# Softmax rows scaled at the evacuation of x instead of at P, by way of DRAM

## The chip, the cores and the metric

The kernel runs on one core of a Trainium2 chip. The metric is the device time of one execution in microseconds (us). The core has TensorE (PE, with its weight loads PEld), VectorE (DVE), ScalarE (ACT), GpSimd (POOL), and SyncE (SP), which in this kernel issues nearly all DMA transfers.

## The reference

Attention with a threshold for 8 batches of 8 heads (576 rows, head size 64), whose output x (4608 x 512) goes through a feed-forward layer that takes the maximum of three products.

```python
scores = scale * np.matmul(q, k.transpose(0, 1, 3, 2))
thresh = np.max(scores, axis=-1, keepdims=True) - tau          # tau = 0.02
scores = np.where(scores >= thresh, scores, -1000000000.0)
attn = np.exp(scores - np.max(scores, axis=-1, keepdims=True))
attn = attn / (np.sum(attn, axis=-1, keepdims=True) + 1e-09)
x = np.matmul(attn, v)                                          # (B, H, S, D) -> (B*S, H*D)
h = np.maximum(np.maximum(x @ w1, x @ w2), x @ w3)              # w: 512 x 768
out = h @ w_out                                                 # 768 x 512
```

## The kernel before

The work is cut into **quads**: 16 of them, two to a batch, each of four heads (two couples r = 0, 1). A quad's rows come as nine chunks (idx 0 to 8) of 128 rows; a chunk has two halves of 576 columns, one for each r. So there are 288 halves and 144 chunks. In the last batch (SPLIT) the rows are worked off in two parts.

A half goes through these steps. `scores` multiplies q and k on PE into a PSUM bank (sc). `maximum` on DVE copies it to a tile z and takes the row's minimum of the negated scores (nm). From there the table MASKED decides, one digit for each half:
- 0 and 2: `threshold` (only for 0, a small DVE instruction), then `exponents` on ACT flattens what lies under the threshold, then `numerators` on ACT takes the exponential and its row sum (letter n).
- 1 and 3: `exponents` on ACT takes the exponential, then `numerators` on DVE (SCALAR_TENSOR_TENSOR) masks it and sums the row (letter k).

2 and 3 read the scores from PSUM, 0 and 1 from z. Then `reciprocals` (DVE, one instruction for a chunk) and `normalized` (POOL, one instruction for each half) write P = z times the reciprocal sum in bf16, and `turned` transposes P by DMA into the tile ptq. When all chunks of a quad are there, `product` multiplies v with ptq on PE, once for each r, and x's quarter is copied from PSUM to the tile xt: on DVE for r = 0, on ACT for r = 1. `ffn` makes the hidden pieces of a batch (`hid`: bank ph, 6 x 3 of them; each has two halves on PE, letters F and B; ACT copies the first of three, DVE takes the two maxima) and then the output pieces (`outp`: bank po).

There are four PSUM banks for all of this. z has 9 buffers (ZBUFS) and, from the 73rd half on, also the two buffers of the weight stage (MORE_Z, `half_of_z`); P has 6.

The order on every engine is written out by hand in the string ORDER. A letter issues the next step of its kind, and each engine executes its own instructions in the order in which they appear: S, T, O, F, N (with the number of a bank) are PE's scores, transposes, products, feed-forward pieces and ninth rows; B is the second half of a piece; m maximum, s threshold, e exponents, n and k numerators, r reciprocals, p normalized, t the DMA transpose, a and c the evacuations of q and k, q their swapped copies, w and x the evacuations of x (DVE, ACT), h and v those of the hidden pieces (ACT, DVE), u, j and f those of the output, l, g, o, i, d the loads and stores, y and z POOL's casts. The class `_Ordered` (line 93, the line of nearly all rows of the profile) ties each instruction to the one before it on its engine.

Of the kernel before, what the change touches and what calls it, by code (L numbers as in the profile page):

```python
# [15 lines left out]
OP = AluOpType  # L16
# [5 lines left out]
FLAT = 2.0 ** -100  # L22

MASKED = """
232222322322222222021032222202332122123122200200111000000000100000000011
000010111020011000101000000001100001001000010011111100000000100100000000
110010030111000100010000000001010100001110001011010100110000000000000000
100101101011000000120000001010000000110011100000001110001000010011111021
# [6 lines left out]
MORE_Z = 72  # L35
# [5 lines left out]
llllllglllT0laclT1laclzllqqS0qqS1meS2mS3lmlT0enlkS1ylmlT2eamelrnpS3leqlmnyS1qcapS0emtnrcS3pmnT2qmepgrelS1qya  # L41
gS0pmelT2mqnS3tcpemqS2nlkT1eytaS0rmnT1kpermS3yS2enczrmS1qT0enmepnqtS3nprmaymgpeS0lptS2mppT0mtpS1enencnqsS3re
rmtpS0mS1penmS3lqnsS2mtperpekzllmT0tmpenkT1pgS3eearnS0petmnqrS2meqlnpS3lmnplsS2cetpremS1pS0nmplermtzeS3mnS2p
mtnpmS3rkpS1leektS0emnrpmemptS1eekS2pO3mktS0rennmpermT2pnS1wptemS3prkyO0tmeakS2pgS1enxlnrmS0lpesS2mezT3mS1np
mgntspcS2eqrseT3mtpeS0srmapS1mnT2ptS3mnqO0ceqmeO1prswnptnkS3pxS0meF1meS2zBresmT0qghF3klpF2nkBtaS1sveS0pemF3B
nyrrsmyBepT1svS0hpcT2nS3zmaS1erpgsF2mntpsBmnS3yvF1etssT0myeBprS2cnpS3mnS0ympelF2epF3lmBnzslssvS0htBrqmeS2vpn
S1gF0sepmF3teqBmF2erssvpBtnBkphF0eS1vtS3znmF2nrBmqteS1rpvBnS3pmlnF0pmgeS1qsBsrhmS3pevS2npS1mF0npsO3ermpesmO2
zewepgsskBxtT3nF1vS2nklBarS0mlphS3mtepF2sS1rmnyBmetF3pvT0eBpcnS2tzT1nvS0asmzS3temS2qeS1meF0trkpmS3lenpBmnlys
reklpF1umerpskS3upBeoketmS0uS2umpS3tesmS1qeT0myO2nqlrsnlprcO3etqsmepwS0xptS1mnF3psnmS2BlerskpS1thF0meF3pmeBF
2ktnBveBsrS1nvpS0hmyF3emF2npBrssT0eprtvBaF1kS3nqvBeF0myhyS2kyleF3mBelBvnpS2snsS0vptemS1pnF3rmpT2tnBmpeF0scS1  # L50
htBrnmpF3erT2rpvlBasS1pstvnS2pmeF0pS3emtBqnmT2S1hcqS3empF2eS0rsqmtS1epsmBeF3pmnF0stsvBeBknF2klhF1BvelS0nrvpB
emT3pS2arvS0ptnS3mpnO1smtesrkpeF2swnlrpmeT0S1qtescS3epBmnpmnT0trskS3paS1umS0ulqmeS3lmyS1nopS2smelS0rmeS3psmn
O1ypersmqO2etkpemO0lewqxlknpS3tS1keF2momS3lexF0ktT1enkBercpnsBpumN1ertkphkF3jS0rursS1empBnmF2ptS0vpS1smeF3yt
BsnsmBpnvS0pT1hmF2atT3srepS0cF1eprBsmeqF3vnByBynvplS2nsS0plmhS1mteS2mF0nF3mteS1rrspBnmS2pelvBlepF1smT0leqBvl
aS2rkhF3oqnsS0mtS1epmBeqsF2ssmtS0epvBeyF1mnF3vpBesrS0ktphBermS1npT2svO0nytmpncT3eS1wF2nrmS0aBrsmnqF3vnT1pS0c
eBptsF2mhpS1eS3pmteS0qmBeO1spmnkteF3rvnpT0BsskapS2xvS0erS1qmtnS3pmnF2mqlespmeS1rtkBepresmT3puS1cuS0ptmnS3pS2
meyS1lrekpF0tnsmempO3lekteskO2nrsmpeBkpxrnwS1uptS3muS2pnmF0yoeS1mF3lesymBtnS2srkpS1hmBeF0spveF2ertBmpT3nrsvS
1paBlmpnS0tS3qhmF1epsmS2leBymF3tevF0nBknlS1rsvpS2esmqnBF3srmhpS1epS0tmeF2pssBrempBtesvS0ynF1mT3lnpBvF0lhsrcS
2tnT1mBnF3valS2nrBsqmeF0pvS1epS2meBptsmS3eqF1hmT2peBcS3tnskT2O0arkplnmO2lerpvewptS3xkpS1nF2meF0sstreBsmpS3nv
pBnmS1tS2hmT3eF0rmpnF1cBpnBrevptT3S2apvS0qmtS3S1enmqF2esrsqmiepmleS0soykeS1plBnmemtS3ukS0uT1snrlO2cpekynO1me  # L60
ymeF3pwxskteS0keS1BrrnkopmF2pmS0BqeuurtsmF1phS3srnpS2meT0ptBmeS3ykpaN2esvempF0tS1jkpF3ermBeS2ptvnS1pmBnS0rls
hsmpS2elF3mqntS1mpF0nsrBskpeF2lsmBetBpveF1yhvS3lnkS2lesF0mytnBmBerqsS3veF2lpvnF1pBsmT0htBceF3rT2vnpBsaS0pvnF
1qmtS2nBsrnmT0pS3hrcpF2esS1mpteS0rmpS3emBpntF1svqnS0ssBmpeoT2vO3lamtneF1wS0nrlBpmeS3qsrS2hsmS0pnmF1eptS3smeB
pmF2ntS0veS3rsmnpS1BnpO0veytrempS2empS3xsmS1tekF0nsknlT2rmpBelmlpnscS3quS1umyS2eorT0kpeO3tmeyO1ewlepsmF3etka
rknS2qklT0nBmxespcS2eryF0mpF1uskpuBtnS2BhmqF3nsvS0peS2srmtpF1eBmpeF0srvnBptS2hyS3pmeF1lmeBlBevtF3nkT2S0arrvp
BnS2mphS1smpF0ntS3smnpBmeF1lsT2esvlF3nrBrcptBnvpS2eS0qmlhS1tsnprsmT3F2epmS0aptBemF3yevS1oS0nqmBnpsrS2mnF1ptv
S0epmBeS3mthS2skeF0F1snmlBeklO3ersvpnrmByepF0swT2eqtBvnqF3ssrcS1hpiBmpT0S2vaptS1snmS0pnT3mqF2tecT1BarmS3pnS1
vqeS0mF2pesrmnptmS3npT1seS0qctBeymqermpS1eS3mpuF0nmtuskS1eS2klnS3smBesrsepO1upmemO2txrkpukeO3wnkpS0xS2emF3et
rmS1pnBssspmF2hS0rtepS3mnBpmF1etS0veF3mnN2rnpBpjF0evtF2esBkBkhF1nsvS3eBmBevO3hrkS2pwnS1mnF3prmS2eptsF0mnBpsS
1sevyS2terBmpeF3svS1iyepBmoS0yhmtF2ekF3nBsmS1ersBvpnF0pmeF2BvteS1hBmF3rsS0vpeF1rknpBBmnO2vhptO0xrpnS3pwS2trm  # L70
npS0mnF3pmteF1pBeBvtS0rS2vpS3empF1ktkF0kBereskpemBkperumO2uptO3xpN1wtenkO2jrF3pxF1hpF2nvF3tvF1rhF2pvF3pvF1hF
2tvF3vF1hF2voF3vF1ohF2vF3vF1hF2vO3vO1wF2xuuF1oF0hiF3vF1vF0hF3vF1vF0hF3vF1vF0hF3vF1vF0hF3vF1vF0huF3vF1ovF3uoF
0uoN1fjdi
# [31 lines left out]
def kernel(  # L105
# [44 lines left out]
    def weight_loads():  # L150


        def piece(dst, src):
            my = {}

            def load():
                my["t"] = stage.tile([128, 4 * 256], F32, name="stage")
# [19 lines left out]
    small = ctx.enter_context(tc.tile_pool(name="small", bufs=6))  # L177
# [177 lines left out]
    halves_of_z = iter(range(1 << 20))  # L355

    def half_of_z():

        n = next(halves_of_z)
        if n >= MORE_Z and (n - MORE_Z) % (ZBUFS + 2) >= ZBUFS:  # L360
            return stage.tile([128, 4 * 256], F32, name="stage")[:, :S]
        return zz.tile([128, S], F32, name="z")

    def maximum(c, r):

        z = c["z", r] = half_of_z()
# [8 lines left out]
    def threshold(c, r):  # L375
        th = c["th", r] = small.tile([128, 1], F32, name="th", bufs=5)
        vector.tensor_scalar(out=th, in0=c["nm", r], scalar1=-1.0, scalar2=tau, op0=OP.mult, op1=OP.subtract)
# [22 lines left out]
    def normalized(c):  # L400
        c["P"] = P = pp.tile([128, W], BF16, name="P")
        for n in range(2):
            pool.tensor_scalar(out=P[:, n * S:(n + 1) * S], in0=c["z", n],
                                    scalar1=c["rs"][:, n:n + 1], scalar2=1.0, op0=OP.mult, op1=OP.mult)
            if n:
                line["t"].append(c)
            yield
# [7 lines left out]
    def product(L, r, target, part=None):  # L415
# [26 lines left out]
        def on_vector():  # L442
            ps = st["ps"]
            dst = target(L["b"])[:, 2 * L["qd"] + r, :]
            vector.tensor_copy(out=dst[:, lo:hi], in_=ps[:, base:base + hi - lo])

        def on_scalar():
            ps = st["ps"]
            dst = target(L["b"])[:, 2 * L["qd"] + r, :]
            scalar.activation(out=dst[:, lo:hi], in_=ps[:, base:base + hi - lo], func=AF.Copy)  # L450
        p = _Piece((L["b"], L["qd"], r, part), first)
        p.vector = on_vector if r == 0 else None
        p.scalar = on_scalar if r == 1 else None
# [25 lines left out]
    def ffn(b, part):  # L479
# [87 lines left out]
        def ninths_of_two():  # L567
# [11 lines left out]
            def done():  # L579
                ob = hp_.tile([128, DM], F32, name="ob9", bufs=1)  # L580
# [12 lines left out]
        def ninth():  # L593
# [10 lines left out]
            def done():  # L604
                ob = hp_.tile([128, DM], F32, name="ob9", bufs=1)[:, 0:DM // 2]
# [36 lines left out]
    Ls, xts, stores, stores9, ends, ninths = {}, {}, [], [], [], []  # L642
# [20 lines left out]
    vector.memset(vrs[2], 0.0)  # L663
    for t in vrs[0:2]:
# [33 lines left out]

    def flow(what, fn):
        while True:  # L700
            yield from fn(line[what].pop(0))
# [5 lines left out]
                O=products(), F=pieces(), N=iter(lambda: ninths.pop(0), None))  # L707
    line = {k: [] for k in "menkrptahvuxwcqsjf"}
    casts = iter([w[1] for w in wl])
    loads = iter([w[0] for w in wl])  # L710
    flows = dict(p=flow("p", normalized), q=flow("q", lambda x: swapped(*x)),
# [7 lines left out]
    def issue(what, where):  # L719
# [10 lines left out]
        elif what == "O":  # L730
            p = next(todo["O"])
            p.first(where)
            for k, fn in (("x", p.scalar), ("w", p.vector)):
                if fn:
                    line[k].append(fn)
# [11 lines left out]
        elif what == "m":  # L747
            c, r = line["m"].pop(0)
            maximum(c, r)
            line["e"].append((c, r))  # L750
            if not masked(c["g"], c["idx"], r) and not direct(c, r):
                line["s"].append((c, r))
        elif what == "s":
            threshold(*line["s"].pop(0))
# [4 lines left out]
        elif what in "nk":  # L759
            c, r = line[what].pop(0)  # L760
# [69 lines left out]
```

## Time and profile before

| | |
|---|---|
| time, median of three runs | 447.64 us (447.23, 447.64, 447.99) |
| profiled execution: span from first to last instruction | 444.8 us (a time of its own is not listed for it) |
| PE busy | 422.4 us (95%) |
| DVE / ACT / POOL busy | 392.8 / 403.0 / 311.9 us |
| DMA | 88.5 MB, mean 199 GB/s |

How to read the rows: a group row has line, engine, operation, the tiles written and read, shapes and count; then the time in which the group was busy, the mean of one instruction in ns, and the idle time in front of them with what ended it. A timeline row has start, duration and instruction. A row of busy time by stretch has its length and, for each engine, busy time and count, then the granted clock of TensorE, the DMA engines' busy share (over 1 when transfers overlap) and GB/s. A DMA row has tiles, issuing engine, count, size and the median time from issue to landing. SPq is SP's queue: an instruction that issues a DMA.

### The profile page before, as it was taken

The page shows a single profiled execution, that of the slowest core. Times are in us where ns is not written, and L with a number is a line of the kernel's source. Part 1 is how long each engine was busy: PE and PEld are TensorE (multiplying, and loading weights), DVE is VectorE, ACT ScalarE, POOL GpSimd, SP SyncE. Part 2 cuts the span into 40 slices and gives each one's busy share as a digit, 9 for nine tenths or more (in the row PEclk, how much of TensorE's full clock was granted, in tenths as well). Part 3 has the DMA queues.
Part 4 walks back from the last instruction along what each step waited for, and adds up shares of the span by engine and source line. Part 5 has one row for each costly group of instructions (what it writes and reads, how often), then busy time and mean ns, then how long its engine had stood idle before and what let it go on. Part 6 is the DMA issues. An engine that isn't in the chain of part 4 may idle for free.

```text
span 444.8 us, 14254 instructions
## 1 busy us (share of the span) xinstructions
PE 422.4 (95%) x5188; PEld 320.2 (72%) x5190; DVE 392.8 (88%) x1228; ACT 403.0 (91%) x836; POOL 311.9 (70%) x420
## 2 busy tenths in 40 slices
PE   7767789999999999999999999999999999999996
PEld 6334347787788767787788777788688886787873
DVE  3887999999999999999999999998999998899642
ACT  3999999999999999999999999899999999987632
POOL 2799989997878687696785877676676685457400
PEclk8998999999999999999999999999999999999999
DMA  7999999999999999699899999989999977487633
GB/s 188 275 293 199 291 169 269 235 243 262 229 180 194 212 222 292 125 256 167 143 234 189 230 198 203 209 168 210 208 206 194 244 151 105 83 179 136 145 116 108
DMA packets 213959, 88.50 MB, mean 199 GB/s; under 512 B 189184, under 2 KB 202240, under 8 KB 213888
## 3 DMA queue, kind: packets, MB, share of 16 engines
q1 hardware_dynamic: 213360, 86.96, 95.9%
q8 instruction: 41, 0.67, 0.6%
q10 hardware_dynamic: 528, 0.62, 0.5%
q14 instruction: 30, 0.25, 0.2%
HBM read 35.65 MB, written 9.44 MB: 101 GB/s over the span
## 4 chain that ended last, share of the span: by engine, by line
PE 86%; ACT 5%; DVE 4%; issue 2%; DMA 1%; SPq 0%; DVEq 0%; ACTq 0%
PE ph L93 32%; PE sc L93 32%; PE po L93 10%; PE o L93 9%; ACT z L93 5%; PE tp L93 3%; DVE z L93 3%; DMA qm<-in_q_dram 1%; ACT qt L93 1%; SPq L93 0%; DVE xt L93 0%; DVE hm L93 0%; DVE stage L93 0%; DVE rs L93 0%; ACT ob L93 0%
## 5 line engine op out<-in xcount | busy, mean ns | idle before, releaser
L93 POOL TENSOR_SCALAR P<-z,rs 128x576 bf16<-128x576 f32 x250 | 200.6, 814 | 63.3 <-DVE rs L93 28.1
L93 DVE TENSOR_SCALAR_CACHE_REDUCE z<-sc 128x576 f32<-128x576 f32 x250 | 183.7, 750 | 14.8 <-PE sc L93 10.1
L93 PE MATMUL sc<-kt,qs 64*128 64x256 f32 (+2 forms) x640 | 182.6, 423 | 5.7 <-DVE z L93 2.3
L93 PE MATMUL sc<-kt,qt 64*128 64x320 f32 (+2 forms) x640 | 182.4, 433 | 5.2 <-ACT z L93 3.3
L93 PE MATMUL ph<-xt,w 64*128 64x288 bf16 (+2 forms) x2160 | 170.8, 283 | 0.1
L93 PEld LDWEIGHTS <-w 64*128 64x128 bf16 (+1 forms) x2160 | 130.1, 94 | 28.6 <-issue 4.3
L93 ACT ACTIVATE z<-z 128x576 f32<-128x576 f32 x174 | 117.6, 679 | 0.1
L93 PEld LDWEIGHTS sc<-kt,qs 64*128 64x128 f32 (+1 forms) x640 | 92.4, 180 | 25.7 <-DVE z L93 5.7
L93 ACT ACTIVATE z<-z,th 128x576 f32<-128x576 f32 x143 | 106.2, 769 | 5.0 <-DVE th L93 4.2
L93 PEld LDWEIGHTS sc<-kt,qt 64*128 64x128 f32 (+1 forms) x640 | 91.9, 179 | 19.7 <-ACT z L93 5.9
L93 DVE SCALAR_TENSOR_TENSOR z<-z 128x576 f32<-128x576 f32 x76 | 62.2, 830 | 0.5 <-ACT z L93 0.5
L93 PE MATMUL po<-wo,hT 64*128 64x512 bf16 (+3 forms) x454 | 53.5, 354 | 0.3
L93 POOL COPY qs<-qt 64x640 f32<-64x640 f32 (+3 forms) x66 | 43.0, 652 | 10.8 <-ACT qt L93 7.2
L93 ACT ACTIVATE z<-z,nm 128x576 f32<-128x576 f32 x68 | 50.6, 767 | 0.0
L93 DVE TENSOR_TENSOR hm<-ph,hm 128x576 bf16<-128x576 f32 (+2 forms) x54 | 37.0, 686 | 9.2 <-PE ph L93 8.9
L93 ACT ACTIVATE hm<-ph 128x576 bf16<-128x576 f32 (+2 forms) x54 | 31.8, 589 | 13.4 <-PE ph L93 12.8
L93 POOL TENSOR_SCALAR P<-stage,rs 128x576 bf16<-128x576 f32 x38 | 30.4, 804 | 19.3 <-ACT z L93 5.4
L93 PEld LDWEIGHTS <-hT 64*128 64x128 bf16 (+2 forms) x456 | 30.0, 95 | 16.5 <-issue 2.3
L93 DVE TENSOR_TENSOR hT<-ph,hm 128x576 bf16<-128x576 f32 (+2 forms) x54 | 37.0, 686 | 4.0 <-PE ph L93 2.3
L93 PE MATMUL o<-ptq,vb 128*64 128x64 bf16 (+2 forms) x544 | 39.0, 281 | 0.0
L93 ACT ACTIVATION_READ_ACCUMULATOR z<-z 128x1 f32 x174 | 34.3, 197 | 0.0
L93 PEld LDWEIGHTS <-vb 128*64 128x64 bf16 x544 | 23.3, 111 | 12.8 <-issue 4.9
(45 smaller groups left out, 431.6 us busy)
## 6 DMA issues: line engine op xcount, KB each, us to landing
vm<-in_v_dram SPq DMA_DIRECT2D x32, 256.0 KB, 4.8
qm<-in_q_dram SPq DMA_DIRECT2D x15, 512.0 KB, 5.0
km<-in_k_dram SPq DMA_DIRECT2D x15, 512.0 KB, 5.3
out_dram<-ob SPq DMA_DIRECT2D x14, 512.0 KB, 4.0
stage<-in_moe_w_dram SPq DMA_DIRECT2D x9, 512.0 KB, 5.2
ptq<-P SPq DMA_TRANSPOSE x144, 4.0
vr<-in_v_dram SPq DMA_DIRECT2D x16, 128.0 KB, 3.4
stage<-in_moe_w_out_dram SPq DMA_DIRECT2D x3, 512.0 KB, 4.9
```

The source lines that it names most:

```text
L93: ins = fn(*a, **kw)
```

## The change

P stays unscaled. `numerators` write their result straight into P in bf16 (on ACT or DVE), `reciprocals` are taken once for a quad (once for each part in the last batch), in a DVE tile `turn` that DVE turns in blocks of 32 x 32. The result is stored to DRAM (`scale_rows`, letter D), read back by two transfers so that 64 partitions each hold the same row of factors (`scale_tile`, letter R, into a buffer of the weight stage), and multiplied in when x is copied from PSUM, on DVE for both r (letter w). `normalized` on POOL (p), the copy on ACT (x) and the further z buffers of the stage are gone; the small output tile ob9 now uses a z buffer. A mode 4 (`by_pool`) is added to the code, but the new MASKED has no 4: its digits are 164, 87, 28 and 9 of 0, 1, 2, 3 (169, 78, 33 and 8 before). MASKED and ORDER are new throughout.

```diff
     def numerators(c, r):
-        z, acc = c["z", r], c["sm"][:, r:r + 1]
-        if masked(c["g"], c["idx"], r):
-            vector.scalar_tensor_tensor(out=z, in0=z, scalar=thr, in1=z,
+        z, p, acc = c["z", r], half_of_p(c, r), sum_of(c, r)
+        if by_pool(c, r):
+            scalar.activation(out=p, in_=z, func=AF.Exp, bias=c["nm", r], scale=-1.0, accum_out=acc)
+        elif masked(c["g"], c["idx"], r):
+            vector.scalar_tensor_tensor(out=p, in0=z, scalar=thr, in1=z,
                                         op0=OP.is_ge, op1=OP.mult, accum_out=acc)
         else:
-            scalar.activation(out=z, in_=z, func=AF.Exp, scale=-1.0 / FLAT, accum_out=acc)
-    def reciprocals(c):
-        c["rs"] = small.tile([128, 2], F32, name="rs")
-        vector.reciprocal(c["rs"], c["sm"])
-    def normalized(c):
-        c["P"] = P = pp.tile([128, W], BF16, name="P")
-        for n in range(2):
-            pool.tensor_scalar(out=P[:, n * S:(n + 1) * S], in0=c["z", n],
-                                    scalar1=c["rs"][:, n:n + 1], scalar2=1.0, op0=OP.mult, op1=OP.mult)
...
+            scalar.activation(out=p, in_=z, func=AF.Exp, scale=-1.0 / FLAT, accum_out=acc)
...
+    turns = [one.tile([128, 2, 32], F32, name=f"turn{x}") for x in range(2)]
+    def reciprocals(g, part, n):
+        L, t = Ls[g], turns[n % 2]
...
+        if part is None:
+            vector.reciprocal(new[:, :, f:f + 9], sums[:, :, f:f + 9])
...
+            vector.reciprocal(new[to, :, at:at + 1], sums[of, :, was:was + 1])
+        vector.transpose(t[:, 1, :], t[:, 0, :])
+        scales[g, part] = dict(t=t)
+    def scale_rows(g, part):
+        s = scales[g, part]
+        s["rows"] = rows.tile([32, 128], F32, name="rows")
+        sync.dma_start(out=s["rows"].rearrange("j (b t) -> b j t", b=4), in_=s["t"][:, 1, :])
+    def scale_tile(g, part):
+        s, (lo, hi) = scales[g, part], span(part)
+        n = hi - lo
+        s["R"] = stage.tile([128, W], F32, name="stage").rearrange("p (r n) -> p r n", r=2)[:, :, 0:n]
+        src = s["rows"].rearrange("j t -> (j t)")[0:2560].rearrange("(r i y) -> i r y", i=2, y=640)
+        o = 64 * ninth_first(Ls[g]["b"]) + lo
+        for i in range(2):
+            sync.dma_start(out=s["R"][64 * i:64 * i + 64],
+                           in_=src[i, :, o:o + n].unsqueeze(0).to_broadcast([64, 2, n]))
...
-        def on_vector():
-            vector.tensor_copy(out=dst[:, lo:hi], in_=ps[:, base:base + hi - lo])
-        def on_scalar():
-            scalar.activation(out=dst[:, lo:hi], in_=ps[:, base:base + hi - lo], func=AF.Copy)
+        def done():
+            vector.tensor_tensor(out=dst[:, lo:hi], in0=ps[:, base:base + hi - lo],
+                                 in1=scales[2 * L["b"] + L["qd"], part]["R"][:, r, :], op=OP.mult)
```

In the new ORDER a unit (a quad, or a quad's part in the last batch; 18 of them) has the letters r, D and R in this order, then O and w. Two passages of it, the 15th unit from its D on and the last one:

```
DsRnesevS0S3mtO1eemF2tBw
rvtF3tF1F0hvF3vF1F2vhF3F0DRvhvF1F3O0vovO3wwF1F0F2
```

More of the change, by code (lines that the diff above doesn't have):

```diff
@@ L353, in direct, with by_pool @@
         return by_mask[2 * number[c["g"], c["idx"]] + r] in "23"
[L355 to L362, printed above, removed]
+    def by_pool(c, r):
+        return by_mask[2 * number[c["g"], c["idx"]] + r] == "4"
     def maximum(c, r):
-        z = c["z", r] = half_of_z()
+        z = c["z", r] = zz.tile([128, S], F32, name="z")
         nm = c["nm", r] = small.tile([128, 1], F32, name="nm")
@@ L663 @@
     vector.memset(vrs[2], 0.0)
+    for t in turns:
+        vector.memset(t[:, 0], 1.0)
     for t in vrs[0:2]:
@@ L697, in products, with units @@
                         yield product(Ls[g], r, x_of, part)
+    def units():
+        n = 0
+        for b in range(B):
+            for part in parts_of(b):
+                for g in (2 * b, 2 * b + 1):
+                    yield g, part, n
+                    n += 1
     def flow(what, fn):
@@ L753, in issue @@
         elif what == "s":
[L754 removed]
+            c, r = line["s"].pop(0)
+            threshold(c, r)
+            if by_pool(c, r):
+                line["b"].append((c, r))
+        elif what == "b":
+            c, r = line["b"].pop(0)
+            set_apart(c, r)
+            line["X"].append((c, r))
         elif what == "e":
@@ L758, in issue @@
             line["k" if masked(c["g"], c["idx"], r) else "n"].append((c, r))
-        elif what in "nk":
-            c, r = line[what].pop(0)
-            if "sm" not in c:
-                c["sm"] = small.tile([128, 2], F32, name="sm")
-            else:
-                c["summed"] = True
-            numerators(c, r)
-        elif what == "r":
-            c = made[line["r"].append(0) or len(line["r"]) - 1]
-            assert c["summed"]
-            reciprocals(c)
-            line["p"].append(c)
+        elif what in "nkX":
+            numerators(*line[what].pop(0))
+        elif what == "r":
+            g, part, n = next(todo["r"])
+            reciprocals(g, part, n)
+            line["D"].append((g, part))
+        elif what == "D":
+            g, part = line["D"].pop(0)
+            scale_rows(g, part)
+            line["R"].append((g, part))
+        elif what == "R":
+            scale_tile(*line["R"].pop(0))
         elif what == "t":
```

144 lines of the change are left out of this document (84 added, 60 removed).

## The prediction

> **What bounds the kernel now.** I read the page first: the busy shares, the 40 slices, the chain that ended last.
>
> ```profile
> span 444.8 us, 14254 instructions
> PE 422.4 (95%) x5188; PEld 320.2 (72%) x5190; DVE 392.8 (88%) x1228; ACT 403.0 (91%) x836; POOL 311.9 (70%) x420
> PE   7767789999999999999999999999999999999996
> ...
> PE ph L93 32%; PE sc L93 32%; PE po L93 10%; PE o L93 9%; ACT z L93 5%; PE tp L93 3%; DVE z L93 3%; DMA qm<-in_q_dram 1%; ACT qt L93 1%; SPq L93 0%; DVE xt L93 0%; DVE hm L93 0%; DVE stage L93 0%; DVE rs L93 0%; ACT ob L93 0%
> ```
>
> The slices say where PE is not busy: the first seven and the last. Then the busy time by stretch, which puts microseconds on that.
>
> ```profile
> core 0: us, PE busy (x) PEld busy (x) DVE busy (x) ACT busy (x) POOL busy (x), PEclk, DMA share, GB/s
> 9.00:75.00 66.00, 52.07 (x475) 30.41 (x475) 58.34 (x176) 63.59 (x137) 58.23 (x77) 0.93 1.12 249
> 0.00:89.00 89.00, 72.23 (x723) 46.57 (x725) 73.79 (x229) 79.96 (x171) 72.36 (x102) 0.94 1.08 240
> ...
> 89.00:433.00 344.00, 342.74 (x4420) 269.48 (x4418) 316.18 (x995) 320.10 (x661) 239.51 (x319) 1.00 0.97 192
> ...
> 200.00:300.00 100.00, 99.00 (x1295) 77.63 (x1292) 95.44 (x302) 96.46 (x199) 73.11 (x98) 1.00 1.02 193
> ...
> 433.00:445.00 12.00, 7.44 (x50) 4.15 (x49) 2.88 (x6) 2.94 (x6) 0.00 (x0) 0.98 0.29 100
> ```
>
> PE idles 89.0 - 72.23 = 16.8 us before 89 us, 1.3 us in the 344 us after it, and 4.6 us at the end. The change adds no matmul and removes none, so PE's 422.4 us stay. Only those 22 us can shrink, and any new hold shows as new PE idle time. In the front (9 to 75 us) ACT is busy 63.6 of 66 us (96%), DVE 88%: ACT feeds PE there. The order of PE's pieces is nearly the old one: the first hidden piece comes after score 54 in both, hidden piece 18 after score 79 in both.
>
> **What the change takes away and adds, engine by engine.** The groups give the counts, the timeline the time from one start to the next, which is what an operation costs on a full engine (its record overlaps the next one's).
>
> ```profile
> L93 POOL TENSOR_SCALAR P<-z,rs 128x576 bf16<-128x576 f32 x250 | 200.6, 814 | 63.3 <-DVE rs L93 28.1 <-ACT z L93 11.6 <-DVE th L93 7.4
> L93 DVE SCALAR_TENSOR_TENSOR z<-z 128x576 f32<-128x576 f32 x76 | 62.2, 830 | 0.5 <-ACT z L93 0.5
> L93 DVE TENSOR_TENSOR hm<-ph,hm 128x576 bf16<-128x576 f32 x42 | 31.5, 751 | 0.8 <-PE ph L93 0.6
> L93 DVE RECIPROCAL rs<-sm 128x2 f32<-128x2 f32 x144 | 22.0, 157 | 2.0 <-ACT z L93 1.4 <-ACT stage L93 0.2
> L93 DVE CAST xt<-o 128x576 bf16<-128x576 f32 x14 | 10.5, 749 | 0.5 <-PE o L93 0.5
> L93 ACT ACTIVATE xt<-o 128x576 bf16<-128x576 f32 x14 | 9.0, 640 | 0.2
> ```
>
> ```profile
> 11.57 0.76 DVE L93 SCALAR_TENSOR_TENSOR z<-z 128x576 f32<-128x576 f32 x1
> ...
> 12.26 0.75 DVE L93 TENSOR_SCALAR_CACHE_REDUCE z<-sc 128x576 f32<-128x576 f32 x1
> ...
> 64.33 0.75 DVE L93 TENSOR_SCALAR_CACHE_REDUCE z<-sc 128x576 f32<-128x576 f32 x1
> ...
> 64.47 0.67 ACT L93 ACTIVATE z<-z 128x576 f32<-128x576 f32 x1
> ...
> 65.01 0.75 DVE L93 TENSOR_SCALAR_CACHE_REDUCE z<-sc 128x576 f32<-128x576 f32 x1
> ...
> 65.14 0.67 ACT L93 ACTIVATE z<-z 128x576 f32<-128x576 f32 x1
> ...
> 66.48 0.15 DVE L93 RECIPROCAL rs<-sm 128x2 f32<-128x2 f32 x1
> 66.56 0.13 DVE L93 TENSOR_SCALAR th<-nm 128x1 f32<-128x1 f32 x1
> ...
> 72.37 0.64 ACT L93 ACTIVATE xt<-o 128x576 bf16<-128x576 f32 x1
> ...
> 72.90 1.44 ACT L93 ACTIVATE z<-z,nm 128x576 f32<-128x576 f32 x2
> ...
> 73.06 0.67 PE L93 MATMUL ph<-xt,w 64*128 64x288 bf16 x8
> ```
>
> So an unmasked numerator (its sum included) costs ACT 65.14 - 64.47 = 0.67 us; a maximum costs DVE 65.01 - 64.33 = 0.68, a masked numerator 12.26 - 11.57 = 0.69, a reciprocal 0.08; an evacuation of x costs ACT 72.90 - 72.37 = 0.53.
> - POOL loses all 288 scalings (250 at 814 ns and 38 on the stage tile). It is on no chain, so this alone is worth nothing.
> - ACT loses 18 evacuations (16 of full width, 9 us) and 10 unmasked numerators (n: 202 to 192; 6.7 us).
> - DVE loses 144 reciprocals (11.5 us), gains 18 groups of two or three reciprocals and a turn (not in the trace; between 0.16 and 0.48 us each by the reciprocal's row, taken as 0.25: 4.5 us), 18 evacuations with a multiplication (like hm<-ph,hm, 0.751 us beside the cast's 0.749, so no dearer than a cast; 0.68 each: 11 us) and 10 masked numerators (7 us). The masked numerator's mean of 830 ns against 760 for an undisturbed one should fall when POOL is quiet (-6 us). In sum +5 us for DVE, -16 for ACT. Neither bounds after 89 us, so there it only adds slack.
>
> In the front it counts. Up to the 72nd score the old order has 51 unmasked numerators, 2 evacuations of x and 4 of hm on ACT; the new one has 43, none and 5: 8 x 0.67 + 2 x 0.53 - 0.53 = **5.9 us less ACT work**. DVE there: masked numerators 15 to 21 (+4.1), evacuations 2 to 4 (+1.4), reciprocals 32 to three groups (-1.8), one maximum fewer (-0.7), quieter POOL (-1): +2 us. ACT had about 89 us of work to that point (67 exponents and 51 numerators at 0.67, 18 evacuations at 0.53) and DVE about 78 (71 maxima and 36 further passes at some 0.68, 54 small ones at 0.08); now it is 83 and 80, so DVE is next, 3 us behind. Bounds of the gain: 5.9 us if both run without gaps, about 2 if two equally full engines lose 5% to waiting for each other. I take **-4.5 us**.
>
> **The new chain.** For each of 18 units (a quad, or its part in the last batch): reciprocals, a store of 16 KB (D), two reads of 295 KB (R), then the evacuation (w) on DVE, which is executed in order: everything queued behind w (maxima, masked numerators, the maxima of the hidden pieces) stands still until both reads have landed, and PE's four banks are not freed. D and R go through SP, also in order: R, 36 issues, sits there until D has landed, and the transposes and loads behind it wait too.
>
> ```profile
> vm<-in_v_dram SPq DMA_DIRECT2D x32, 256.0 KB, 4.8
> ...
> km<-in_k_dram SPq DMA_DIRECT2D x15, 512.0 KB, 5.3
> ...
> out_dram<-ob SPq DMA_DIRECT2D x6, 128.0 KB, 3.4
> out_dram<-ob SPq DMA_DIRECT2D x3, 256.0 KB, 2.4
> ...
> out_dram<-ob SPq DMA_DIRECT2D x3, 64.0 KB, 2.6
> ```
>
> ```profile
> 66.99 0.66 SPq L93 DMA_DIRECT2D stage<-in_moe_w_dram  x1
> ```
>
> ```profile
> L93 SPq DMA_TRANSPOSE ptq<-P x144: 1241/1432/4678, 17.6 to 418.9; - x144
> ...
> DMA to landing us min/median/max: 3.2/4.0/8.1
> ```
>
> ```profile
> SPq L93 <- POOL P L93: 130.9, 83, 6.0
> ```
>
> Neither transfer is in the trace. D: nearest is the 64 KB store, 2.6 us (2.4 to 3.4 by the stores). R: nearest is vm's 256 KB load, 4.8 us; a transpose of the same 295 KB has median 4.0, at least 3.2; the upper bound is km's 5.3. The second read is issued 0.66 us after the first. From D's start to usable factors: 2.6 + 0.66 + 4.4 = **7.7 us**, bounds 2.4 + 0.66 + 3.2 = 6.3 and 3.4 + 0.66 + 5.3 = 9.4. The issues' SP time (54 x 0.66 = 36 us) and the waits for D (18 x 2.6 = 47 us) fit into what SP no longer waits for POOL (130.9 us).
>
> What covers the 7.7 us is PE's work between D and w in the new order. By the chain's shares a score is 32% of 444.8 / 288 = 0.49 us, a half of a hidden piece as much (288 of them), a product 9% / 36 = 1.1 us, a half of an output piece about 1.3 us (10% over 28 such halves and nine single pieces). Counting letters, twelve units have 7 us or more (the first four among them, as PE idles there), and POOL's absence hurts nowhere. Short ones:
> - unit 15, "DsRnesevS0S3mtO1eemF2tBw": two scores, a product, two halves: 3.1 us. D can run at most 0.5 us ahead of its place, since a store stands before it. DVE is held 7.7 - 3.6 = 4.1 us.
> - unit 12: three scores, an output half, a product, 4 us; only the reciprocals stand before D, so it can go 2.4 us early: held 1.2. Unit 5: 6.3 us by DVE's own work: held 1.4. Units 9 and 14: covered within 0.4 us.
>
> What a hold costs PE is in the trace: one masked numerator took 2.60 us, and the only hole in PE's middle lies right there.
>
> ```profile
> 277.13 2.60 DVE L93 SCALAR_TENSOR_TENSOR z<-z 128x576 f32<-128x576 f32 x1
> ```
>
> 1.9 us more than 0.69 on DVE went with the 1.0 us that PE misses between 200 and 300 us, so about 0.9 us of a hold is absorbed. Unit 15 then costs 3.2 us, units 5 and 12 together 0.8: **+4.0 us**.
>
> - The tail (unit 18, "DRvhvF1F3O0vovO3ww"). Nothing but the last part's hidden pieces follows, and they need x.
>
> ```profile
> 423.77 0.61 PE L93 MATMUL o<-ptq,vb 128*64 128x256 bf16 x8
> ...
> 424.58 1.47 PE L93 MATMUL po<-wo,hT 128*128 128x512 bf16 x5
> 424.69 0.44 ACT L93 ACTIVATE xt<-o 128x320 bf16<-128x320 f32 x1 [2.02 <-PE o L93]
> ```
>
> Today the output piece (424.58, 1.47 us) hides the evacuation. After: from D, two hidden pieces (0.9), two products (1.6), the output piece (1.3): 3.8 us, plus up to 1.5 if SP has issued the last transpose ahead of its place. Needed: 7.7 and two evacuations of 0.4. 8.5 - 5.3 = **+3.2 us** of PE idle, with nothing to absorb it. Bounds: 1.8 (chain 6.3) to 6.4 (chain 9.4, SP not ahead).
>
> - Transposes behind a waiting R. Four products follow their quad's last transpose by 2.1 to 2.9 us of PE work in the new order (the least before was 3.9), against 4.0 us to landing. But P is now ready without POOL's two scalings, so SP can issue earlier than the order's place. 0 to +4; taken as **+0.3**. z has 9 buffers instead of 11, but is free after the numerators instead of after POOL: nothing.
>
> Sum: -4.5 + 4.0 + 3.2 + 0.3 = **+3.0 us**. The profiled execution spans 444.8 us, 2.8 under the median of the three times, 447.64; what lies around the span stays. So 447.8 for the span and **450.6 us** for the time.
>
> The Trainium skill, "DMA: Bandwidth & Descriptors", section "Anatomy of one DMA — SWDGE (gpsimd) path", gives 2.0 us plus bytes at 436 GB/s for a transfer issued from GpSimd; as an estimate for D and R, 2.0 + 0.66 + 2.7 = 5.4 us. The rows above (2.6 and 4.8) are above it and decide; by it the time would be that of the first rival. The same section warns that completion is slow above all when the target is HBM, which speaks against this change.
>
> **Rivals.** About 0.9 us (0.2%) is what a measurement can tell from no change.
> 1. Faster: the chain is at its lower bound (6.3 us) and SP, no longer held by POOL for 130.9 us, runs D ahead of its place. Unit 15 costs 6.3 - 3.6 - 0.9 = 1.8, or 0.5 with D at its reciprocals; the tail 1.0 to 1.8; the front gives 5 to 5.9. -2 to -4.4: **443 to 445.6**, centre 444.3. For it: transposes land in 3.2 us where DMA is light, which includes the tail. Against: DMA's share is 0.97 in the middle. It decides from a chain under 6.5 us. Chance 0.37.
> 2. Much slower: store and reads queue behind transposes and loads, the chain takes 9.4 us, and most units hold. Unit 15: 4.9; unit 12: 2.0; unit 5: 2.2; units 9 and 14: 1.2 each; the tail 5; three more units at 8 us of cover 0.5 each; late transposes 2: +20 - 4.5 gives up to 463; with half of that **453 to 460**. For it: a transpose's 8.1 us at worst and a DMA share of 1.12 in the front. Against: the median of 4.0. Chance 0.12. The skill's same page, "Why a DMA increments its semaphore by 16 and not by 1", lets a transfer run on the largest number of engines, up to 16, that divides both slowest dimensions, which for D (4 and 128) is four engines; no row here shows it.
> 3. No change: gain and loss cancel, or the order hides all and the front stays bound by DVE: 447.6 within 0.9. Chance 0.07.
>
> **How the numbers follow.** My forecast has 0.44 (448.6 to 454). Slower by over 0.2%: 0.44 + 0.12 = 0.56; within: 0.07; faster: 0.37. The range leaves a tenth out at each end: 442 to 456.
>
> **What would show it.** Right: the first hidden piece some 4 to 5 us earlier than 73.06 us; ACT and DVE both above 93% in the front; waits "DVE xt <- DMA" of 3 us or more at two or three places, PE idle there and a hole of about 3 us before the last part's hidden pieces; SP waiting for the store's landing. Wrong: no DMA wait of DVE over 1 us (rival 1), or such waits in most units (rival 2); D landing well off 2.6 us or the reads off 4.4.

## The result and the profile after

The changed kernel takes 497.3 us (median of four, 493.4 to 501.5) against 447.8 us: a ratio of 1.108, 95% interval 1.101 to 1.116, so **slower by some 48 us**. One of the four, at 501.5 us, is over 1.5% above the fastest and is not in the ratio. The forecast was 450.6 us (442 to 456), with up to 463 for the worst rival. The direction was the likelier one; the size was missed by a factor of sixteen.

The page of the profiled execution after: its span, the busy shares, the slices of PE and of the DMA engines, the chain.

```profile
span 492.3 us, 13683 instructions
...
PE 443.2 (90%) x5188; PEld 302.2 (61%) x5190; DVE 407.3 (83%) x1173; ACT 393.0 (80%) x798; POOL 88.9 (18%) x132
...
PE   7858689968999997999989999979999999999986
...
DMA  7999999999999899989999989959698996793932
...
PE 58%; DMA 19%; DVE 9%; ACT 5%; issue 4%; SPq 3%; POOL 1%; ACTq 0%; DVEq 0%; POOLq 0%
PE ph L89 28%; PE sc L89 19%; DMA stage<-rows 9%; PE po L89 5%; PE o L89 4%; DVE z L89 4%; DMA ptq<-P 3%; SPq L89 3%; PE tp L89 2%; DMA stage<-in_moe_w_dram 2%; ACT z L89 2%; DMA rows<-turn 2%; ACT P L89 2%; DVE P L89 1%; DVE xt L89 1%
```

Before, the only transfer listed on the chain was a load of q, 1%. Now DMA has 19%, and the reads of the factors 9% of the span. PE's 443.2 us have the same 5188 matmuls as the 422.4 us before; the ends of matmuls are modelled in this profile, so busy time of PE can hold short stalls. The stretches:

```profile
9.00:75.00 66.00, 49.96 (x470) 30.42 (x466) 58.62 (x168) 57.84 (x121) 24.09 (x33) 0.95 1.11 251
0.00:89.00 89.00, 70.52 (x722) 46.55 (x722) 74.72 (x223) 73.77 (x152) 27.04 (x43) 0.96 1.06 236
89.00:433.00 344.00, 319.83 (x3895) 218.42 (x3893) 296.78 (x854) 290.19 (x587) 61.82 (x90) 0.98 0.97 202
200.00:300.00 100.00, 95.24 (x1202) 64.89 (x1198) 91.05 (x264) 85.54 (x172) 17.90 (x28) 1.00 1.00 203
112.00:118.00 6.00, 5.01 (x28) 3.74 (x28) 4.34 (x10) 2.16 (x4) 2.47 (x3) 0.50 1.15 264
```

In the 344 us of the middle PE now idles 24.2 us (1.3 before) and gets through 3895 matmuls where it had done 4420. In the front it has done 722 matmuls by 89 us, as before (723): no gain is left. ACT and DVE are busy 57.84 and 58.62 of the 66 us from 9 to 75 (88% and 89%, both forecast above 93%), and the first hidden piece starts at 72.2 us against 73.06, not 4 to 5 us earlier. What is waited for, from the waits of the changed kernel (total us, times, longest):

```profile
PEld L89 <- PE ph L89: 31.5, 84, 0.6
ACT hm L89 <- PE ph L89: 30.3, 32, 4.1
DVE xt L89 <- DMA stage<-rows: 29.3, 12, 6.1
...
POOL w L89 <- DMA stage<-in_moe_w_dram: 24.7, 7, 10.9
...
PEld L89 <- issue: 17.4, 50, 1.4
...
PEld sc L89 <- DVE xt L89: 11.8, 6, 4.0
...
ACT P L89 <- DMA ptq<-P: 5.4, 5, 2.1
```

Two new rows stand out. DVE waits for the factors twelve times, where two or three were forecast, but most of that does not reach PE, which waits for that evacuation only about 12 us. And PE's weight loads wait 84 times, some 0.375 us each, for PE itself (ph): a hidden piece's second half opens with a gate that waits for the first half's last matmul, and in the new ORDER the B stands directly behind its F for 90 of 140 pieces (84 hidden, 6 output); in the old one for 1 of 140.

The worst single place is unit 3. SP's issues (timeline):

```profile
90.31 0.59 SPq L89 DMA_DIRECT2D rows<-turn  x1
...
92.67 7.93 SPq L89 DMA_TRANSPOSE ptq<-P  x4
...
102.51 1.00 SPq L89 DMA_DIRECT2D qm<-in_q_dram  x1
106.98 1.24 SPq L89 DMA_DIRECT2D stage<-rows  x2
```

DVE and PE there:

```profile
112.18 1.42 DVE L89 TENSOR_TENSOR xt<-o,stage 128x576 bf16<-128x576 f32 x2 [6.07 <-DMA stage<-rows]
```

```profile
112.99 0.90 PE L89 MATMUL sc<-kt,qs 64*128 64x320 f32 x1 [3.82 <-DVE xt L89]
```

The store is issued at 90.3 us, and the reads only at 107.0: behind four transposes (about 2 us of SP each), loads, and the stage buffer that the weights still use (SP waits 2.4 us for a weight's load there). DVE stands 6.1 us, PE 3.8, and then the granted clock is 0.50 from 112 to 118 us (the row above).

The trace's DMA totals show how full the queue already was. The main queue: packets, MB, and the time its packets took as a share of 16 engines' span, before and after:

```profile
q1 hardware_dynamic: 213360, 86.96, 95.9%
```

```profile
q1 hardware_dynamic: 220920, 96.70, 93.0%
```

Before, 95.9% of 444.8 us = 426.6 us; after, 93.0% of 492.3 = 457.8 us. The DMA engines' own time after is longer than the whole span before.

### The profile page after: what moved, and what is told of

Its sections match the earlier page's. It is cut to its first block, busy times and chain, and to the rows that moved or that the text cites. A ratio compares the mean times of both kernels' runs of the same rounds, so it can differ in the third digit from the quotient of the medians.

```text
span 492.3 us, 13683 instructions
## 1 busy us (share of the span) xinstructions
PE 443.2 (90%) x5188; PEld 302.2 (61%) x5190; DVE 407.3 (83%) x1173; ACT 393.0 (80%) x798; POOL 88.9 (18%) x132
## 3 DMA queue, kind: packets, MB, share of 16 engines
q1 hardware_dynamic: 220920, 96.70, 93.0%
## 4 chain that ended last, share of the span: by engine, by line
PE 58%; DMA 19%; DVE 9%; ACT 5%; issue 4%; SPq 3%; POOL 1%; ACTq 0%; DVEq 0%; POOLq 0%
PE ph L89 28%; PE sc L89 19%; DMA stage<-rows 9%; PE po L89 5%; PE o L89 4%; DVE z L89 4%; DMA ptq<-P 3%; SPq L89 3%; PE tp L89 2%; DMA stage<-in_moe_w_dram 2%; ACT z L89 2%; DMA rows<-turn 2%; ACT P L89 2%; DVE P L89 1%; DVE xt L89 1%
## 5 line engine op out<-in xcount | busy, mean ns | idle before, releaser
L89 DVE TENSOR_SCALAR_CACHE_REDUCE z<-sc 128x576 f32<-128x576 f32 x288 | 208.9, 750 | 18.5 <-PE sc L89 11.9
L89 PE MATMUL ph<-xt,w 64*128 64x288 bf16 (+2 forms) x2160 | 178.9, 286 | 7.8 <-DVE xt L89 1.5
L89 PEld LDWEIGHTS <-w 64*128 64x128 bf16 (+1 forms) x2160 | 111.5, 95 | 64.8 <-PE ph L89 31.5
L89 ACT ACTIVATE z<-z,th 128x576 f32<-128x576 f32 x164 | 121.7, 766 | 17.2 <-DVE th L89 16.8
L89 ACT ACTIVATE P<-z 128x576 bf16<-128x576 f32 x192 | 129.0, 674 | 5.7 <-DMA ptq<-P 5.4
L89 DVE SCALAR_TENSOR_TENSOR P<-z 128x576 bf16<-128x576 f32 x96 | 75.6, 794 | 0.4 <-DMA ptq<-P 0.3
L89 ACT ACTIVATE z<-z,nm 128x576 f32<-128x576 f32 x87 | 65.2, 765 | 0.1
L89 DVE TENSOR_TENSOR xt<-o,stage 128x576 bf16<-128x576 f32 (+2 forms) x36 | 24.3, 687 | 33.1 <-DMA stage<-rows 29.3
L89 DVE TENSOR_TENSOR hm<-ph,hm 128x576 bf16<-128x576 f32 (+2 forms) x54 | 37.1, 687 | 11.9 <-PE ph L89 10.2
L89 ACT ACTIVATION_READ_ACCUMULATOR P<-z 128x1 f32 x192 | 36.8, 192 | 0.0
L89 ACT ACTIVATE qt<-tp 128x640 f32<-128x640 f32 (+3 forms) x34 | 21.0, 616 | 18.4 <-PE tp L89 18.1
```

Source lines behind the costliest of these rows:

```text
L89: ins = fn(*a, **kw)
```

## The experiments

Ratios are to the kernel before, measured on the same chip, with 95% intervals. Where the factors are replaced by a constant, reciprocals and turn stay unless said otherwise.

**1. Halves separated; the trip left out; both.** In `e_sep`, 71 letters B move behind the next piece of PE, after which no B stands directly behind its F. In `e_const` D and R do nothing and x is multiplied by a constant tile. `e_sep_const` has both.

```diff
-...S0sF3qBnmesS2mzS1tesF0kmBhmesteT3ktanvF2S1eBT3F0...
+...S0sF3qnmesS2BmzS1tesF0kmhmesteT3BktanvF2S1eBT3F0...
```

> The changed kernel with one edit of the order: 71 letters B are moved behind the next piece on PE, so that no piece has its two halves next to each other (90 of 140 pieces have in the changed kernel, 1 of 140 before). Theory H (halves): PE's weight loads wait 31.5 + 4.6 us for the first half's end in 93 places, because the second half starts by waiting for the first; with another piece between them these waits go. H expects 494 us to fall by 25 to 36, to 458 to 469. Theory R (round trip): the loss is DVE's 29.3 us of waiting for the factors and what follows from it; R expects 485 to 494.

> The changed kernel in its own order, without the store and the reads: x is multiplied by a constant tile instead of the factors read back from DRAM (the row scaling is left out). H expects 475 to 488 (DVE's holds go, the waits between halves stay). R expects 450 to 465.

> Both edits: halves separated, and x multiplied by a constant tile (the row scaling is left out). H expects 440 to 450: what is left is the forecast's gain in the front. R expects the same as without the separated halves, within 5 us. If both are wrong about the rest (P's six buffers, nine buffers of z, SP), this stays above 455.

Measured: e_sep 498.4 us, 1.117 (1.115 to 1.119); e_const 472.3 us, 1.059 (1.055 to 1.062); e_sep_const 477.9 us, 1.072 (1.067 to 1.078). The trip through DRAM costs 1.108 - 1.059 = 5.0%, **22 us**; the other 26 us are there without it. Separating the halves gave nothing: neither with the trip nor without it did the time fall. The waits of e_sep:

```profile
PEld L89 <- issue: 26.8, 71, 1.3
```

The waits "PEld <- PE ph" of these weight loads (31.5 us) are gone. Those for which the profile shows no releaser grew from 50 (17.4 us, in the waits of the changed kernel) to 71 (26.8 us), so some 22 us of these waits have really gone, and the time has not followed: in this order they were not what the time hung on.

**2. Halves together in the kernel before.** `b_adj` pulls 79 letters B to their F, so that 84 of 140 stand together; nothing else changes.

```diff
-...S0meF1meS2zBresmT0qghF3klpF2nkBtaS1...
+...S0meF1BmeS2zresmT0qghF3BklpF2nktaS1...
```

> The kernel before with one edit of the order: the letter B is moved right behind its F for 79 pieces, so that 84 of 140 pieces have their halves next to each other; nothing else changes and no work is added. H expects 447.8 to rise by 20 to 32 us, to 468 to 480, with waits of the weight loads for PE's hidden pieces of some 30 us. R expects 446 to 450.

Measured: 475.0 us, 1.064 (1.063 to 1.066). Its waits:

```profile
PEld L93 <- PE ph L93: 28.8, 78, 0.4
```

28.8 us of waits, and the time is 28.5 us longer. In the old order this costs in full.

**3. The change's code in the old order.** `old_order` takes the old MASKED and ORDER, drops p, turns x into w, and puts r and D at each unit's last numerator and R some 3 us of PE work later, with 8.6 to 24 us of cover. `old_const` is the same with a constant for the factors.

```
...BsnrDsmBnvS0T1hmF2atT3seS0cF1ReBsmeqF3vnByBynvlS2...
```

> The change in the order of before: code of the changed kernel, MASKED and ORDER of before, in ORDER without p, with w for x, and for each unit r and D behind its last numerator and R 3 us of PE work later. Halves apart as before (1 of 140 adjacent); from D to the end of the first product lie 8.6 to 24 us of PE work. Theory H (the order, above all its adjacent halves, costs the 47 us; the round trip costs where it is uncovered) expects 443 to 452. Theory R (the round trip and P's and z's shorter supply of buffers cost, in whatever order) expects 465 or more.

> The same without the store and the reads: x is multiplied by a constant tile (the row scaling is left out). H expects 441 to 449, within 4 us of the same order with the round trip, since its cover is 8.6 us and more. R expects at least 15 us less than with the round trip.

Measured: old_order 504.9 us, 1.129 (1.127 to 1.132); old_const 474.1 us, 1.064 (1.059 to 1.069). Even with ample cover and apart halves it is slower than the change: the trip costs 6.5% (29 us) here, and something else 6.4% (some 28 us). In old_order's waits there is no large wait for the factors at all:

```profile
ACT P L89 <- DMA ptq<-P: 19.1, 13, 4.2
...
DVE z L89 <- DMA out_dram<-z: 11.1, 3, 6.5
DVE P L89 <- DMA ptq<-P: 8.9, 3, 5.3
```

What waits are the numerators, for one of P's six buffers, which is free when its transpose has landed, and maxima, for a z that an output store still reads. In old_const these waits are small:

```profile
ACT P L89 <- DMA ptq<-P: 3.8, 3, 1.8
```

**4. Stores and reads that nobody waits for.** `e_unread` issues every D and R of the change, but x is multiplied by a constant.

> The changed kernel in its own order; the store and the reads are issued as ever, but x is multiplied by a constant tile and the factors read back are used by nobody (the row scaling is left out). If the 22 us between the changed kernel and the one without the transfers are DVE's holds, this comes out at 470 to 476. If they are SP's queue and the DMA engines' load, it stays at 488 to 494.

Measured: 490.7 us, 1.099 (1.095 to 1.103), about 4 us under the change: most of the trip's 22 us stay when DVE waits for none of it. Its waits:

```profile
ACT P L89 <- DMA ptq<-P: 20.3, 11, 3.7
```

**5. Which part of that traffic.** `e_early` reads factors that were stored once at the start, so that no read waits for a store; `e_half` reads one of the two rows; `e_poolq` issues D and R from GpSimd's queue; `b_copy` adds 36 copies of 288 KB to the kernel before.

```diff
-        src = s["rows"].rearrange("j t -> (j t)")[0:2560]...
+        src = fixed.rearrange("j t -> (j t)")[0:2560]...                 # e_early
-            sync.dma_start(out=s["R"][64 * i:64 * i + 64], in_=src[i, :, o:o + n]...
+            sync.dma_start(out=s["R"][64 * i:64 * i + 64, 0:1], in_=src[i, 0:1, o:o + n]...   # e_half
+            pool.dma_start(out=s["R"][64 * i:64 * i + 64], in_=src[i, :, o:o + n]...   # e_poolq
+            sync.dma_start(out=spare, in_=q[0]...)                       # b_copy, at each O
```

> The changed kernel, with every read taking its factors from rows stored once at the start (all ones), and each unit's store still issued, unread; so no read waits for a store, on SyncE or on VectorE, and all bytes stay. The row scaling is left out. Theory SP: 476 to 484, SyncE no longer stands at a read (11.9 us in six waits after the change, and what the waits for the stage buffer add). Theory DMA: 488 to 496.

> The changed kernel, with each read of the factors fetching one of its two rows, so half the bytes by as many issues; both evacuations use that row (the other row's factors are left out). The factors add some 54 us of time on the 16 DMA engines (93.0% of 492.3 us against 85.7% of 471.2 us without the trip), where before they were at 95.9% of 444.8 us. Theory DMA (the added bytes don't fit in): 482 to 488, half of the trip's 22 us comes back. Theory SP (the issues and the wait for the store hold what is behind them): 491 to 498, no change.

> The changed kernel, with the store of the factors and its two reads issued from GpSimd's queue instead of SyncE's, at the same places. Theory SP (SyncE, in order, stands at a read until the store has landed, and transposes and loads queue behind it): 474 to 482, most of the 22 us that the trip costs come back, and the waits of ScalarE for P's buffers fall from 5 us to under 2. Theory DMA (the DMA engines are too busy, whoever issues): 490 to 497, with the reads' 5.3 us to landing unchanged. Theory GpSimd (its casts of v and w now stand behind the store): slower than the change, above 500.

> The kernel before, with one copy of 288 KB from DRAM to DRAM issued by SyncE at each of the 36 products, read by nobody: the bytes of the factors and their issues, and nothing else of the change. Theory DMA: the DMA engines had 4.1% of 444.8 us left, 18 us, and the copies ask for some 54: 460 to 480, and transposes and loads land later. If the DMA engines' 95.9% is elastic and what is late is off the path: 447 to 452. SyncE's 36 issues of 0.66 us alone, 24 us, fit into its 130.9 us of waiting.

Measured: e_early 491.4 us, 1.102 (1.095 to 1.108), hardly different from the change. e_half 484.5 us, 1.085 (1.080 to 1.091): half the bytes give back 10 of the 22 us. e_poolq 503.2 to 518.7 us in four runs, too far apart for an interval; GpSimd's queue does not bring the time back. Its waits, from the execution of 513.2 us, show GpSimd standing where SP had stood:

```profile
POOL rows L89 <- DVE turn L89: 68.3, 9, 12.0
POOL stage L89 <- DMA rows<-turn: 45.3, 14, 5.3
DVE xt L89 <- DMA stage<-rows: 38.4, 9, 7.1
```

The Trainium skill, "DMA: Bandwidth & Descriptors", section "Issuing engines are not separate DMA queues", says that transfers of all issuing engines run on the same 16 DMA engines and that another issuer saves issue time alone; the run agrees in that no time came back. b_copy 455.9 us (median of three; a fourth took 2374.6 us), 1.020 (1.014 to 1.025): bytes and issues alone, in an order that waits for none of them, cost 9 us, which lies between the two expectations. The main queue's row of e_const, e_half and b_copy:

```profile
q1 hardware_dynamic: 213360, 86.96, 85.7%
```

```profile
q1 hardware_dynamic: 218616, 91.98, 91.6%
```

```profile
q1 hardware_dynamic: 214512, 97.58, 100.2%
```

As time of the DMA engines: e_const 85.7% of 471.2 us = 404, e_half 91.6% of 481.8 = 441, after 458, b_copy 100.2% of 455.5 = 456. In b_copy the DMA engines are full over the whole span, and the kernel still loses only 9 us. In the change they are not full on average (93.0%). So a full queue alone does not make the loss; what differs is who waits for a landing. Summed from the waits of each profiled execution, in us:

| run | ratio | DVE, for the factors | ACT and DVE, for P's buffers | DVE, for a z that a store reads | sum |
|---|---|---|---|---|---|
| e_const (no trip) | 1.059 | 0 | 7.1 | 2.3 | 9.4 |
| e_half | 1.085 | 13.1 | 5.4 | 4.4 | 22.9 |
| e_unread | 1.099 | 0 | 21.4 | 4.7 | 26.1 |
| e_early | 1.102 | 24.1 | 2.9 | 3.1 | 30.1 |
| the change | 1.108 | 29.3 | 5.7 | 3.3 | 38.3 |
| old_const (no trip) | 1.064 | 0 | 4.6 | 3.6 | 8.2 |
| old_order | 1.129 | 0 | 28.0 | 11.1 | 39.1 |

In each order the time rises with the sum, as far as the intervals tell the runs apart, and where DVE does not wait for the factors, the numerators wait for P's buffers instead. In the kernel before, ACT and DVE have no such wait: GpSimd writes P there, and even in b_copy it waits only 4.1 us for transposes (and DVE 12.4 us for a z that GpSimd still reads, 2.6 before). Why P comes free later is not separated. The transposes' median from issue to landing hardly moves (4.4 us in old_const, 4.5 in old_order; 4.1 in e_const, 4.5 after, but 4.2 in e_early), so a later issue by SP is as possible as a slower transfer.

**6. What else the change takes, in the old order without the trip.** `oc_z11` gives old_const the 11 z buffers and ob9's own tile back (the turns are left out to make room, 3.8 us of DVE as listed, and the constant is an immediate); `oc_z11_x` also puts every second evacuation of x back on ACT; `oc_nor` leaves out the reciprocals too. `es_z11` gives 11 z buffers to e_sep_const.

```diff
-        z = c["z", r] = zz.tile([128, S], F32, name="z")
+        z = c["z", r] = half_of_z()
...
-                ob = zz.tile([128, S], F32, name="z")[:, 0:DM]
+                ob = hp_.tile([128, DM], F32, name="ob9", bufs=1)
```

> The old order with a constant factor (row scaling left out), but with the 11 score buffers of before (nine of z and the two of stage) and a buffer of its own for the output tile of the ninth chunks; the 18 turns are left out too, about 3 us of VectorE. With nine buffers this order took 474.1 us against 447.4 before. Theory Z (the maxima find no free score buffer, since the change took two of the eleven and put five output tiles in among the nine): 448 to 455, the waits of the maxima for an output store gone and TensorE's idle time back from 33.9 to 22 to 26 us. Theory X (VectorE has got all evacuations of x): 468 to 474. Theory M (any retiming of a hand-tuned order loses some 25 us in many short waits): 468 to 476, with the idle time spread over VectorE and ScalarE as before.

> As the one with 11 score buffers, and every second evacuation of x is again on ScalarE at its old place. Row scaling is left out. Theory Z: no further gain, within 3 us of the one with 11 buffers. Theory X: 448 to 455 here alone. Theory M: still 465 or more, since what stays of the change is that exponents are written straight into P, one reciprocal group in place of eight, and a quiet GpSimd.

> The old order with 11 score buffers, x on both engines and a constant factor, as in the run that took 456.9 us, now without the 18 groups of reciprocals too (row scaling and row sums' reciprocals are left out). What stays of the change: numerators written straight into P, no scaling by GpSimd, no reciprocals. Theory r (the reciprocals stand right behind the last numerator in VectorE's order and hold it for ScalarE, 6.8 us in 12 waits with nine buffers): 447 to 451. Theory P (the numerators take a buffer of P that a transpose must free first, on engines that can't wait): 454 to 459, no change.

> The changed kernel in its own order, with separated halves, a constant factor (row scaling left out) and the 11 score buffers of before instead of 9. With nine it took 477.9 us. Theory Z (score buffers are what the separated order runs out of): 455 to 466, VectorE's waits at the maxima and TensorE's idle time for them (11.5 us) mostly gone. Theory M (this order is timed for other durations, buffers or not): 472 to 480.

Measured: oc_z11 460.5 us, 1.029 (1.026 to 1.032); oc_z11_x 456.9 us, 1.023 (1.018 to 1.028); oc_nor 450.1 us, 1.008 (1.006 to 1.010). From old_const's 1.064 these are steps of 3.5% (score buffers, ob9 and turns), 0.6% (x on DVE, within the intervals) and 1.5% (reciprocals); 0.8% are left. With the trip's 6.5% they make up old_order's 12.9%. oc_z11_x's waits show the reciprocal group, which stands right behind a unit's last numerator on DVE and waits for ACT to finish it:

```profile
DVE turn L90 <- ACT P L90: 9.6, 13, 2.2
```

es_z11 472.4 us, 1.060 (1.056 to 1.063): the buffers give 1.3% in the new order, and 26 us remain there.

**7. The front's gain alone.** `b_front4` and `b_front6` take the kernel before and turn four or six unmasked numerators of the front into masked ones on DVE, at the same place: MASKED digits 2 to 3, letters n to k.

> The kernel before, with four score halves of the front (25, 33, 43 and 46 of 288) masked on VectorE at the same place in the order instead of unmasked on ScalarE: the one thing of the change that its front gained by, alone. If the front is bound by ScalarE as read (96% against VectorE's 88% between 9 and 75 us): 4 x 0.67 us less there, 445 to 446.5. If two engines that wait for each other lose it again: 447 to 448.5, no change or a little slower.

> The same with six halves (18, 25, 30, 38, 43, 46). If ScalarE binds: 444 to 446. If VectorE is next at once (88% + 6%): no better than with four, or slower than before.

Measured: b_front4 450.4 us, 1.009 (1.006 to 1.012); b_front6 452.7 us, 1.015 (1.013 to 1.018). Both are slower than before, by 0.9 and 1.5%. The front of b_front4, and with it ACT's relief:

```profile
9.00:75.00 66.00, 47.87 (x450) 27.82 (x448) 59.14 (x178) 60.79 (x128) 60.39 (x76) 0.97 1.16 255
```

ACT is busy 60.8 us instead of 63.6, as planned, and PE lists 450 matmuls instead of 475, in the fastest of its executions (447.7 us). No kernel tried here beats the one before.

## Why the prediction was wrong, point by point

- **The trip's traffic, put at nothing (the step that failed first).** Of the 48 us the trip makes 22; the points on z, on the order and on the reciprocals bear on the other 26. The forecast priced the trip as latency, a chain of 7.7 us in front of DVE (+4.0, +3.2 and +0.3 us), and set SP's issues and waits against SP's 130.9 us of waiting for POOL. Its load on the other transfers was no term of the sum; the DMA shares of 0.97 and 1.12 served only to weigh rivals. Measured: the trip costs 22 us in the new order and 29 in the old one; half the bytes cost about half (e_half), and some 18 us remain when nobody waits for the factors (e_unread), where ACT and DVE stand 21.4 us for P's buffers instead. Adding up bytes would have warned, and no more: 426.6 us x 96.70 / 86.96 MB = 474 us of DMA time in a span of 444.8, but by the same working b_copy would take 479 us, and it took 455.5. The same 86.96 MB took 427 us before and 404 in e_const, and the bytes alone cost the kernel before 9 us. That they cost two to three times as much in the changed kernel goes with the waits of the table above; what makes P's buffers late stays open. SP's time did not come free either: its waits for POOL are gone, but the profile now has 45.0 us of waits for ACT's P and 97.6 for ACT's z; for the store's landing it waits 11.9 us in 6 places, where 47 were priced.
- **"z has 9 buffers instead of 11 ... nothing" (failed).** In the old order z, ob9 and turns cost 3.5%, some 15 us; the turns are at most 3.8 of them.
- **"The order of PE's pieces is nearly the old one" (failed).** I compared where pieces stand among the scores and not B against F. 84 gates wait 31.5 us; in the old order such gates cost 28.5 us (b_adj). But that this is what the new order loses by is not shown: e_sep has no such pair and gains nothing. What in the order costs the 26 us is open.
- **Front, -4.5 us (failed).** The maximum of half 38 does come 5.2 us earlier than before (48.8 against 53.9 us), that of half 66 at the same time (89.7, 89.8), that of half 80 12 us later: units 1 to 3, held as the next point shows, fall between; and alone the shift of numerators makes the kernel slower (by 0.9% for four). So ACT's 96% did not mean that less work on ACT shortens the front. Units 1 to 4 were counted as covered, "as PE idles there": but DVE was held 3.1, 3.1, 6.1 and 0.8 us there.
- **The holds, +4.0 us (wrong places).** Evacuations of units 1, 2, 6 and 15 on DVE:

```profile
53.92 0.76 DVE L89 TENSOR_TENSOR xt<-o,stage 128x576 bf16<-128x576 f32 x1 [3.06 <-DMA stage<-rows]
...
70.25 0.76 DVE L89 TENSOR_TENSOR xt<-o,stage 128x576 bf16<-128x576 f32 x1 [3.11 <-DMA stage<-rows]
...
189.17 0.76 DVE L89 TENSOR_TENSOR xt<-o,stage 128x576 bf16<-128x576 f32 x1 [3.96 <-DMA stage<-rows]
...
430.30 0.42 DVE L89 TENSOR_TENSOR xt<-o,stage 128x256 bf16<-128x256 f32 x1 [0.30 <-PE ph L89]
```

Unit 15, forecast as held 4.1 us, waited for no factors; units 3, 6, 2 and 1 were held 6.1, 4.0, 3.1 and 3.1. Units that the forecast took as covered make 22.8 of the 29.3 us. The count of twelve units with 7 us or more of cover was too kind: at the prediction's own prices seven have it from D to w (3, 7, 10, 11, 13, 16, 17). And the cover was counted in PE work, while SP reaches R late: in unit 3, with 13.5 us of such work, 16.7 us passed from D to R. Nor does 0.9 us of each hold vanish: for the holds of 3.1, 6.1 and 4.0 us PE stood 2.9, 3.8 and 3.4. The parts were priced near: 5.3 us for the reads (4.4), 4.5 for a transpose (4.0); the store's landing is not listed.
- **The tail, +3.2 us (right mechanism, price too high).** DVE waits for the factors there as forecast, 2.9 us, D's chain taking 472.82 - 466.43 = 6.4 us in a tail where DMA is light; PE's hole is 1.1 us, since PE had work until 472.25, 5.8 us after the store and not the forecast 3.8 to 5.3.

```profile
466.43 0.56 SPq L89 DMA_DIRECT2D rows<-turn  x1
468.48 1.30 SPq L89 DMA_DIRECT2D stage<-rows  x2
```

```profile
472.82 0.89 DVE L89 TENSOR_TENSOR xt<-o,stage 128x320 bf16<-128x320 f32 x2 [2.93 <-DMA stage<-rows]
```

```profile
473.37 6.82 PE L89 MATMUL ph<-xt,w 128*128 128x320 bf16 x49 [1.12 <-DVE xt L89]
```

- **DVE's small terms.** With a quiet POOL, and now writing bf16, the masked numerator fell from 830 to 794 ns, not to the forecast 760. Reciprocals and turns are listed with 7.0 and 3.8 us against 22.0, about half, where two fifths were forecast (4.5 of 11.5). Of ACT's 18 evacuations 14 are of full width, not 16, which moves nothing. What was not priced is where the reciprocals stand: 1.5% in the old order.
- **Rival 2** had the right mechanism (store and reads queue behind transposes and loads, most units held) and the sign, with too small a price: beside DVE's holds it had 2 us for late transposes, where the numerators' waits for P's buffers alone reach 21.4 us in e_unread and 28.0 in old_order (5.7 in the change, where DVE's holds come first).

What stays open: the new order without the trip, with separated halves and 11 z buffers, still takes 472 us, and no run tells which of its properties cost these 26 us.

## What to carry to other kernels

Before adding transfers, read the DMA queues' total share of the span, as one reads an engine's busy share, and then ask which engine stands at a landing. At 95.9% the same megabytes cost 9 us where GpSimd took the waits for P's buffers, and 22 to 29 where ACT and DVE took them. Taking work from an engine that is on no chain (here POOL's scaling) was worth nothing (oc_nor, without it, is 0.8% slower), and giving its buffers and waits to engines that execute in order (P's six buffers to ACT and DVE, a unit's reciprocals to DVE, the stage to the reads) is a cost that the busy sums don't show. Compare two hand-written orders by what each piece stands directly behind, not only by how far along they are.

## What the hardware showed that I had not expected

- A second half directly behind its first waits about 0.375 us (31.5 us / 84); the same pairs made in the old order waited 28.8 us in 78.
- A hole of 3.8 us in PE was followed by a granted clock of 0.50 over the 6 us of the row above, so it cost more than its length (a score's matmul of 64x320 took 0.74 us there, and 0.43 at 72 us). The Trainium skill, "TensorE: Matmul & The Clock Gate", section "What's actually happening", has the clock halved after an idle window of about 3.4 us; the row agrees.
- The same DMA bytes took 427 us of the 16 engines' time before and 404 in e_const: the DMA engines' busy time is no fixed time per byte. In b_copy it reached 100.2% of the span, and the kernel was 2% slower.
